# ScalarE in the order of the text during the first block, and the third weight piece transferred ahead of the fourth tile

## The chip, the core and the metric

The kernel runs on one core of a Trainium2 chip, in one launch. The metric is device time in microseconds (us), from start to end of the program. A core has five engines that run side by side, each through a queue of its own: TensorE (PE), VectorE (DVE), ScalarE (ACT), GpSimd (POOL) and SyncE (SP), which here only issues transfers. Engines wait for each other by semaphores; an instruction that waits holds up what is queued behind it on its engine.

## The reference

Three stages, each fed by the one before: an attention with decaying state, a dense MLP, and a mixture of experts.

```python
for t in range(S):                                   # attention: B=4, H=8, S=768, D=48
    cur = np.einsum('bhd,bhe->bhde', u[None] * kt, vt)
    y[:, :, t] = np.einsum('bhd,bhde->bhe', rt, state + cur)
    state = wt[:, :, :, None] * state + np.einsum('bhd,bhe->bhde', kt, vt)
...
h = x @ w_in                                         # MLP: 3072 tokens, 384 -> 2048 -> 384
x = (np.maximum(h, 0.0) + alpha * np.minimum(h, 0.0)) @ w_out
...
expert_idx = np.argmax(x @ w_gate, axis=1)           # 8 experts, 384 -> 1024 -> 384
out[mask] = gate_w[mask, None] * (np.maximum(x[mask] @ w1[e], 0.0) @ w2[e])
```

## The kernel before, in words

**Work.** The 3072 tokens are 24 tiles of 128 (numbered from 0 here, so the fourth tile is tile 3). A block is three tiles, so there are eight blocks. The attention is done tile by tile. A block then goes through the MLP in 16 groups of 128 hidden units: the first product `p1` (L617, into the bank `ph`), ScalarE's `gn` (L620), VectorE's `gt` (L622), then a split of `gt` into a high part `gh` (ScalarE, L628) and a low part `gl` (VectorE, L630), and the second product `p2` (L643, into `py`) two groups later. Each product is made of three TensorE products of high and low parts. There are two `ph` banks, so `p1` of a group waits for `gt` of the group two before.

**Weight pieces.** The MLP's weights come as 16 pieces of 768 KB (numbered from 0, so the third piece is piece 2; even ones are of `w_in`, odd ones of `w_out`). They come packed in pairs of words. SyncE's transfer (L199) brings a piece into `raw` (two buffers; piece 2 goes into a tile of its own, `spare`). ScalarE then rebases it with two instructions (L221, L223); VectorE puts the words together with two (L227, L230, tile `v`); ScalarE casts the high part (L243, `wih` or `woh`); VectorE subtracts it for the low part (L247, `wil` or `wol`). Group f needs pieces 2(f//2) and 2(f//2)+1. In the first block this unpacking runs beside the products, one piece for each group.

**Attention of a tile.** VectorE scans the decays (L297), scans back (L322) and scales `k` (L339); TensorE makes scores (L377) and transposes `k` (L402); ScalarE copies scores out (L385, two copies `at`) and the transposed `k` (L407, `kt`), and makes the state's decays `pm` (L368); GpSimd masks the copies (L389), makes a product `rk` for the *next* tile (L344, L345) and `cv` (L357); VectorE sums `rk` to `c` (L350). TensorE's `kv` (L416, L420) needs `kt`. ScalarE and VectorE split the result into `xth` (L470) and `xtl` (L475).

**What sets the order.** The program is written in slots: `at_slot(s, fn)` hangs a stage onto slot s, and the loop over the groups runs slots 2i and 2i+1 at step i. Slots below zero are the prologue, in which the attention of tiles 0 to 2 and the first pieces are done; `PT0` is its start, `PRO_OPS` and `PRO_MOVED` place attention stages in it, and `PRO_W` places the four stages of a piece (rebase, words, high, low). Engines named in `tc.manual_schedule` keep the order in which the text writes their instructions. On all others the framework's scheduler chooses an order at build time, which is then as fixed as the other. `ORDER0 = None` keeps the text's order on every engine in the prologue, `ORDER1` on TensorE and GpSimd from then on, `ORDER2` on TensorE and VectorE near the expert stage. Nothing is reordered when the program runs.

Of the kernel before, what the change touches and what calls it, by code (L numbers as in the profile page):

```python
# [32 lines left out]
NF1 = DFF // 128  # L33
# [14 lines left out]
LAG = 2  # L48
EPE, EDVE = mybir.EngineType.PE, mybir.EngineType.DVE
EACT, EPOOL = mybir.EngineType.Activation, mybir.EngineType.Pool  # L50


ORDER0 = None
ORDER1 = {EPE, EPOOL}
ORDER2 = {EPE, EDVE}
SWITCH = -6

# [21 lines left out]
PT0 = -100  # L79
# [15 lines left out]

PRO_FILL = 27
GATE_CONST = 34
PRO_W = ((15.75, 17, 20.5, 20.6), (19.64, 19.65, 24.3, 24.4), (24.2, 24.3, 100, 101))
PRO_WARM = ((9.6, 6), (11.5, 3), (14.8, 4), (15.65, 3), (21.55, 4), (22, 5))


def s_tile(i):

    blk, j = divmod(i, NB)
    return 2 * NF1 * blk - 10 - (2 * NF1 * (NB - 1 - j)) // NB
# [3 lines left out]
def attention_mlp_moe(ctx, tc, dmaj, tmaj, ub, alpha, w_in, w_out, w_gate, w_gate_b, wexp, out):  # L109
    nc = tc.nc  # L110
    vec, act, pool, pe, sp = nc.vector, nc.scalar, nc.gpsimd, nc.tensor, nc.sync
    order = ExitStack()
# [20 lines left out]
    def load_tile(i):  # L133
        if i < NB:
            both = wp.tile([128, DMW + TMW], F32, tag="W", name="both")
            dm, tm = both[:PR, :DMW], both[:, DMW:]
            if i == 0:
                sp.dma_start(out=dm[:, 1024:], in_=dmaj[i, :, 1024:])
                sp.dma_start(out=dm[:, :1024], in_=dmaj[i, :, :1024])
            else:  # L140
                sp.dma_start(out=dm, in_=dmaj[i])
        else:
            dm = ap.tile([PR, DMW], F32, tag="dm", name="dm")
            tm = ap.tile([128, TMW], F32, tag="tm", name="tm")
            sp.dma_start(out=dm, in_=dmaj[i])
        sp.dma_start(out=tm, in_=tmaj[i])
        dm_t[i], tm_t[i] = dm, tm
# [45 lines left out]
    def wl_dma(j):  # L193
        g, kind = j // 2, j % 2
        if j == 2:
            raw = spare_t[0][:, 1024:2560].bitcast(U32).rearrange("p (n c) -> p n c", c=2)
        else:
            raw = rp.tile([128, 768, 2], U32, tag="raw", name="raw")
        sp.dma_start(  # L199
            out=raw, in_=(w_in if kind == 0 else w_out)[g].bitcast(U32).rearrange("p (n c) -> p n c", c=2)  # L200
        )
        raw_t[j] = raw
# [422 lines left out]
    def p1_out(blk, f):  # L625
        gt = g_t[(blk, f)]
        gh = mp.tile([128, BN], F32R, tag="gh", name="gh", bufs=3)
        act.copy(gh, gt)  # L628
        gl = mp.tile([128, BN], F32R, tag="gl", name="gl", bufs=3)
        vec.tensor_tensor(out=gl, in0=gt, in1=gh.bitcast(F32), op=ALU.subtract)  # L630
        g_t[(blk, f)] = (gh, gl)
# [19 lines left out]
    def p2_out(blk):  # L651
        x2 = mp.tile([128, NB, DM], F32, tag="x2", name="x2", bufs=1)
        for j in range(NB):
            (vec.tensor_copy if j == 1 else act.copy)(x2[:, j, :], y_t[blk][j])
        sp.dma_start(
            out=x2d[BN * blk : BN * (blk + 1), :].rearrange("(j p) d -> p j d", p=128),
            in_=x2,
        )
        return x2
# [64 lines left out]
    def early_table():  # L724
        ti = counts("e")
        vec.tensor_scalar(ti, ti, UNIT.bit_length() - 1, None, op0=ALU.arith_shift_right)
        tf = scratch([1, E], F32, name="tf_e")
        vec.tensor_copy(tf, ti)
        inc = cumulate("e", tf, E)
        yield from unit_table("e", inc, None, iou[:, :EARLY, :], EARLY, E)  # L730
        mn = scratch([1, 1, E + 1], F32, name="mn")
        vec.tensor_scalar(mn, inc, float(EARLY), None, op0=ALU.min)
        tk = scratch([1, E], F32, name="tk")
        vec.tensor_tensor(out=tk, in0=mn[:, 0, 1:], in1=mn[:, 0, :E], op=ALU.subtract)
        rt["taken"] = tk
# [145 lines left out]
    def b_tr(u, q):  # L881
        d = un[u]
        hs = d.pop(("hs", q))
        pt = ps_a.tile([128, 2, 128], F32, tag="pa", name="pht")
        for m in range(2):
            pe.transpose(pt[:, m, :], hs[:, 128 * m : 128 * m + 128], ident)
        pt = pt.rearrange("p m t -> p (m t)")
        gh = qp.tile([128, 256], F32R, tag="gh2", name="ghb", bufs=4)
        act.copy(gh, pt)
        gl = qp.tile([128, 256], F32R, tag="gl2", name="glb", bufs=4)  # L890
        vec.tensor_tensor(out=gl, in0=pt, in1=gh.bitcast(F32), op=ALU.subtract)
        d["g", q] = (gh, gl)
# [15 lines left out]
    def u_out(u):  # L908
        d = un.pop(u)
        for j in range(d["nt"]):  # L910
            ys = qp.tile([128, DM], F32, tag=f"ys{j}", name=f"ys{j}")
            g = d["meta"][:, j, 1:2].bitcast(F32)
            if j == 0:
                act.activation(ys, d["o"][j], AF.Copy, scale=g)  # L914
            else:
                vec.tensor_scalar(ys, d["o"][j], g, None, op0=ALU.mult)
            pool.indirect_dma_start(  # L917
                out=out,
                out_offset=bass.IndirectOffsetOnAxis(ap=d["meta"][:, j, 0:1], axis=0),
                in_=ys,  # L920
                in_offset=None,
                bounds_check=NT - 1,
                oob_is_err=False,
            )
# [20 lines left out]
    def at_slot(s, fn):  # L945
        todo.setdefault(s, []).append(fn)

    def at_slots(s, stages):

        def stage():  # L950
            for _ in stages:
                at_slots(s + 1, stages)
                return

        at_slot(s, stage)

    def run_slot(s):
        for fn in todo.pop(s, ()):
            fn()
# [17 lines left out]
    for i in range(1, NTILE):  # L977
        at_slot(s_tile(i - 2) + 7 if i > NB + 1 else PT0 + 0.1 * i, lambda i=i: load_tile(i))
        if i == NB - 1:
            at_slot(PT0 + 0.1 * i, lambda: wl_dma(0))  # L980
            at_slot(PT0 + 0.1 * i, lambda: wl_dma(1))
            at_slot(PT0 + 0.1 * i, spare)
            at_slot(PT0 + 0.5, lambda: wl_dma(2))
    for j in range(NWL):
        if j < len(PRO_W):
            s = [PT0 + t for t in PRO_W[j]]
        else:
# [32 lines left out]
    for i in range(len(steps) + LAG):  # L1020
        if i == 0:
            order.close()
            tc.no_sync_barrier()
            order.enter_context(tc.manual_schedule(engines=ORDER1))
        if i == NM + SWITCH:
            order.close()
            ctx.enter_context(tc.manual_schedule(engines=ORDER2))
        if i < len(steps):
            kind, b, f = steps[i]
            {"m": p1, "A": u_p1, "B": b_p1}[kind](b, f)  # L1030
        if 0 < i <= len(steps) and steps[i - 1][0] == "B":
            b_tr(*steps[i - 1][1:])
        run_slot(2 * i)
        if i < NM:
            p1_out(*steps[i][1:])
        if i >= LAG:
            kind, b, f = steps[i - LAG]
            {"m": p2, "A": u_p2, "B": b_p2}[kind](b, f)
            if kind == "m" and f == NF1 - 1:
                x2 = p2_out(b)  # L1040
                end = gate_block(b, x2, 2 * i + 1)
                if b == NBLK - 2:
                    at_slot(end + 1, lambda: list(early_table()))
                elif b == NBLK - 1:
                    at_slots(end + 1, final_table())
            elif kind != "m" and f == ulen[kind] - 1:
                u_out(b)
        run_slot(2 * i + 1)
# [87 lines left out]
```

## Time and profile before

| what | value |
| --- | --- |
| runs before | 851.88, 850.15, 851.5 us; median 851.5 |
| the profiled execution | 853.78 us, its span 852.1 us |
| TensorE busy | 807.1 us (95%), granted clock 0.975 of full |
| VectorE busy | 595.3 us (70%) |
| ScalarE busy | 393.9 us (46%) |
| GpSimd busy | 285.5 us (34%) |

The span runs from the first to the last instruction; the execution's own time has some 1.7 us around it. The prologue lasts to about 39 us, the first block from there to about 132 us, the blocks after it to about 620, the experts to the end. A share of busy time is a mean over these stages; what a stage costs is read from its own windows and waits. The granted clock is 1.00 at 2.4 GHz and 0.50 at 1.2 GHz.

### The profile page before, as it was taken

The numbers are of one execution on the slowest core, as the hardware profiler recorded it, in microseconds if no ns is written. First come the engines' busy times: TensorE is split into PE (matmuls) and PEld (weight loads), VectorE is DVE, ScalarE is ACT, GpSimd is POOL, SyncE is SP. The second block draws the span as 40 slices with busy tenths as digits, with TensorE's granted clock in tenths as the row PEclk, the third lists the DMA queues.
The fourth block names the chain that finished last, engine by engine and source line by source line (L and its number), as shares of the span: only waits on it lengthen the run. The fifth ranks groups of instructions, "written<-read, shape, count | busy, mean of one in ns | idle before, by whom it ended". The sixth has DMA issues, their size and how long they took to land. (4 is left out here: it accounts for less than half of the span.)

```text
span 852.1 us, 15696 instructions
## 1 busy us (share of the span) xinstructions
PE 807.1 (95%) x6032; PEld 757.4 (89%) x6032; DVE 595.3 (70%) x1129; ACT 393.9 (46%) x746; POOL 285.5 (34%) x326
## 2 busy tenths in 40 slices
PE   7878979999999999999999999999899999999994
PEld 4667969999999899999989899989899999999993
DVE  5798876467957967967966953546855676767761
ACT  2476744434334243243244333355445566665641
POOL 7762132443324233434324331130433232222301
PEclk9789989999999999999999999999999999999998
DMA  9835652222123122124123200065267577686830
GB/s 275 262 108 184 216 175 95 63 72 90 46 93 67 63 66 74 58 73 121 35 68 92 71 2 29 1 239 217 98 239 256 186 245 273 227 289 204 293 104 20
DMA packets 30516, 114.80 MB, mean 135 GB/s; under 512 B 8229, under 2 KB 11592, under 8 KB 30440
## 3 DMA queue, kind: packets, MB, share of 16 engines
q1 hardware_dynamic: 26088, 103.53, 37.7%
q0 software_dynamic: 4352, 10.26, 3.2%
q8 instruction: 48, 0.79, 0.4%
q14 instruction: 28, 0.23, 0.1%
HBM read 104.11 MB, written 10.45 MB: 134 GB/s over the span
## 5 line engine op out<-in xcount | busy, mean ns | idle before, releaser
L617 PE MATMUL ph<-xth,wih 128*128 128x384 f32 x384 | 135.7, 353 | 11.5 <-DVE gt L622 10.6
L643 PE MATMUL py<-woh,gh 128*128 128x384 f32 x384 | 135.5, 353 | 1.1 <-ACT gh L628 1.0
L628 ACT CAST gh<-gt 128x384 fp32r<-128x384 f32 x128 | 65.7, 514 | 148.5 <-DVE gt L622 147.8
L643 PE MATMUL py<-woh,gl 128*128 128x384 f32 x384 | 130.1, 339 | 3.6 <-DVE gl L630 3.6
L617 PE MATMUL ph<-xth,wil 128*128 128x384 f32 x384 | 129.7, 338 | 3.0 <-DVE wil L247 3.0
L617 PE MATMUL ph<-xtl,wih 128*128 128x384 f32 x384 | 129.4, 337 | 0.0
L643 PE MATMUL py<-wol,gh 128*128 128x384 f32 x384 | 129.3, 337 | 0.0
L622 DVE SCALAR_TENSOR_TENSOR gt<-gn,oma_s,ph 128x384 f32<-128x384 f32 x128 | 77.8, 608 | 56.8 <-ACT gn L620 56.5
L630 DVE TENSOR_TENSOR gl<-gt,gh 128x384 fp32r<-128x384 f32 x128 | 85.8, 670 | 33.7 <-ACT gh L628 31.4
L620 ACT ACTIVATE gn<-ph 128x384 f32<-128x384 f32 x128 | 62.6, 489 | 81.7 <-PE ph L617 78.6
L848 DVE SCALAR_TENSOR_TENSOR gl<-ph,gh 128x256 fp32r<-128x256 f32 x96 | 40.4, 422 | 73.9 <-ACT gh L846 70.0
L389 POOL TENSOR_SCALAR_AFFINE_SELECT at<-at 128x512 f32<-128x512 f32 x46 | 36.8, 821 | 159.9 <-ACT at L385 159.9
L617 PEld LDWEIGHTS ph<-xth,wih 128*128 128x128 f32 x384 | 72.5, 189 | 19.1 <-DVE gt L622 14.3
L843 PE MATMUL ph<-xh,w1h 128*128 128x256 f32 x288 | 81.5, 283 | 2.3 <-DVE gl L848 2.3
L843 PE MATMUL ph<-xh,w1l 128*128 128x256 f32 x288 | 81.2, 282 | 0.0
L917 POOL DMA_INDIRECT out<-ys,meta x28 | 28.2, 1009 | 157.2 <-ACT ys L914 100.2
L843 PE MATMUL ph<-xl,w1h 128*128 128x256 f32 x288 | 80.6, 280 | 0.0
L643 PEld LDWEIGHTS py<-woh,gh 128*128 128x128 f32 x384 | 72.8, 190 | 7.9 <-issue 3.4
L643 PEld LDWEIGHTS py<-woh,gl 128*128 128x128 f32 x384 | 72.8, 189 | 4.7 <-DVE gl L630 4.5
L617 PEld LDWEIGHTS ph<-xth,wil 128*128 128x128 f32 x384 | 72.7, 189 | 3.3 <-DVE wil L247 3.3
L518 DVE SCALAR_TENSOR_TENSOR sink<-x,wgb 128x384 f32<-128x384 f32 x120 | 75.3, 663 | 0.1
L643 PEld LDWEIGHTS py<-wol,gh 128*128 128x128 f32 x384 | 72.9, 190 | 0.0
(219 smaller groups left out, 1860.9 us busy)
## 6 DMA issues: line engine op xcount, KB each, us to landing
raw<-w SPq DMA_DIRECT2D x64, 768.0 KB
tm<-tmaj SPq DMA_DIRECT2D x21, 704.0 KB
dm<-dmaj SPq DMA_DIRECT2D x21, 674.2 KB
raw<-w_out SPq DMA_DIRECT2D x8, 768.0 KB
raw<-w_in SPq DMA_DIRECT2D x7, 768.0 KB
x2d<-x SPq DMA_DIRECT2D x8, 576.0 KB
both<-tmaj SPq DMA_DIRECT2D x3, 704.0 KB
wgb<-w_gate_b SPq DMA_DIRECT2D x2, 768.0 KB
```

What stands on the lines that cost most here:

```text
L389: pool.affine_select(out=cx[jj], in_=cx[jj], pattern=[[0, NP], [1, 128]], compare_op=ALU.is_gt, fill=0.0, base=0, channel_multiplier=-1,)
L518: vec.scalar_tensor_tensor(out=sink, in0=x2[:, j, :], scalar=1.0, in1=wgb_t[h][:, e, :], op0=ALU.mult, op1=ALU.mult, accum_out=cx["l"][:, ...
L617: pe.matmul(ph, lhsT=w, rhs=x[:, c, :], start=k == 0, stop=k == 3 * KC - 1)
L620: act.activation(gn, ph, AF.Relu, scale=-1.0)
L622: vec.scalar_tensor_tensor(out=gt, in0=gn, scalar=oma_s[:, f : f + 1], in1=ph, op0=ALU.mult, op1=ALU.add)
L628: act.copy(gh, gt)
L630: vec.tensor_tensor(out=gl, in0=gt, in1=gh.bitcast(F32), op=ALU.subtract)
L643: pe.matmul(y_t[blk][j], lhsT=g[:, sl], rhs=w, start=f == 0 and m == 0, stop=f == NF1 - 1 and m == 2,)
L843: pe.matmul(ph, lhsT=w, rhs=x, start=k == 0, stop=k == 3 * KC - 1)
L848: vec.scalar_tensor_tensor(out=gl, in0=ph, scalar=0.0, in1=gh.bitcast(F32), op0=ALU.max, op1=ALU.subtract)
L917: pool.indirect_dma_start(out=out, out_offset=bass.IndirectOffsetOnAxis(ap=d["meta"][:, j, 0:1], axis=0), in_=ys, in_offset=None, bounds_c ...
```

## The change

ScalarE joins the engines that keep the text's order, for the first 18 steps of the loop (groups 0 to 15 of the first block, and two more); from step NF1 + LAG = 18 on a new set without it holds, as before. Piece 2 is transferred in the slot of pieces 0 and 1, ahead of tile 3, and its cast and its low part are placed in the prologue (24.5 and 24.6), where they were placed in slots 0 and 1 of the loop.

```diff
-ORDER1 = {EPE, EPOOL}
+ORDER1 = {EPE, EPOOL, EACT}
+ORDER_LATER = {EPE, EPOOL}
...
-PRO_W = ((15.75, 17, 20.5, 20.6), (19.64, 19.65, 24.3, 24.4), (24.2, 24.3, 100, 101))
+PRO_W = ((15.75, 17, 20.5, 20.6), (19.64, 19.65, 24.3, 24.4), (24.2, 24.3, 24.5, 24.6))
...
-            at_slot(PT0 + 0.5, lambda: wl_dma(2))
+            at_slot(PT0 + 0.1 * i, lambda: wl_dma(2))
...
+        if i == NF1 + LAG:
+            order.close()
+            order.enter_context(tc.manual_schedule(engines=ORDER_LATER))
```

The line numbers of the changed kernel are one higher than those above up to the step loop. TensorE's order is the same in both programs. On ScalarE the order changes from the start of the first block on; there it stood so before, with `v_487` piece 3 and `v_529` piece 4:

```order
L221 ACTIVATE v_487<-raw 128x768
L223 ACTIVATE raw<-raw 128x768
L221 ACTIVATE v_529<-raw 128x768
L223 ACTIVATE raw<-raw 128x768
L620 ACTIVATE gn<-ph 128x384
L368 ACTIVATE pm<-bmask,ex 112x96 x4
L628 CAST gh<-gt 128x384
L385 COPY at_532<-pa_504 128x512
L243 CAST woh_124<-v_487 128x768
L620 ACTIVATE gn<-ph 128x384
L385 COPY at_535<-pa_505 128x512
L407 COPY kt<-pk 128x448
```

and now, at the same place on ScalarE, with `v_488` piece 3:

```order
L621 ACTIVATE gn<-ph 128x384
L222 ACTIVATE v_488<-raw 128x768
L224 ACTIVATE raw<-raw 128x768
L629 CAST gh<-gt 128x384
L621 ACTIVATE gn<-ph 128x384
L244 CAST woh_124<-v_488 128x768
L222 ACTIVATE v_529<-raw 128x768
L224 ACTIVATE raw<-raw 128x768
L386 COPY at_532<-pa_504 128x512
L386 COPY at_535<-pa_505 128x512
L629 CAST gh<-gt 128x384
L408 COPY kt<-pk 128x448
```

The first `gn` stands ahead of the rebases, the rebase of piece 4 behind the cast of piece 3, and both copies of the scores and `kt` behind that rebase.

Further on ScalarE, at group 6 and tile 4, before (`v_779` is piece 9, `v_847` piece 10):

```order
L628 CAST gh<-gt 128x384
L620 ACTIVATE gn<-ph 128x384
L407 COPY kt<-pk 128x448
L221 ACTIVATE v_847<-raw 128x768
L243 CAST woh_741<-v_779 128x768
L223 ACTIVATE raw<-raw 128x768
```

and now, from `gh` of group 6:

```order
L629 CAST gh<-gt 128x384
L386 COPY at_815<-pa_787 128x512
L386 COPY at_818<-pa_788 128x512
L621 ACTIVATE gn<-ph 128x384
L244 CAST woh_741<-v_779 128x768
L222 ACTIVATE v_847<-raw 128x768
L224 ACTIVATE raw<-raw 128x768
L408 COPY kt<-pk 128x448
```

`kt` of tile 4 moved from behind `gn` to behind the cast of piece 9 and the rebase of piece 10, and the copies of its scores, which stood a group earlier, to behind `gh`.

VectorE is left to the scheduler in both, and its order changes with ScalarE's. At groups 6 and 7, before (`v_743` is piece 8):

```order
L622 SCALAR_TENSOR_TENSOR gt<-gn,oma_s,ph 128x384
L350 TENSOR_REDUCE c<-rk 128x8
L247 TENSOR_TENSOR wil_740<-v_743,wih_739 128x3x256
L227 SCALAR_TENSOR_TENSOR v_779<-v_779,raw 128x768
L630 TENSOR_TENSOR gl<-gt,gh 128x384
L230 SCALAR_TENSOR_TENSOR v_779<-raw,v_779 128x768
```

and now, from the same `gt`:

```order
L623 SCALAR_TENSOR_TENSOR gt<-gn,oma_s,ph 128x384
L248 TENSOR_TENSOR wil_740<-v_743,wih_739 128x3x256
L228 SCALAR_TENSOR_TENSOR v_779<-v_779,raw 128x768
L631 TENSOR_TENSOR gl<-gt,gh 128x384
L231 SCALAR_TENSOR_TENSOR v_779<-raw,v_779 128x768
L623 SCALAR_TENSOR_TENSOR gt<-gn,oma_s,ph 128x384
L351 TENSOR_REDUCE c<-rk 128x8
```

The sum `c` of tile 5 moved behind the low part of piece 8, the words of piece 9 and the next `gt`.

## Rows read from the trace of the kernel before

**Rows 1.** Windows: busy us of each engine, granted clock, DMA share and GB/s.

```profile
10.00:30.00 20.00, 13.69 (x113) 9.09 (x113) 16.79 (x19) 10.04 (x22) 17.27 (x15) 0.78 1.03 286
50.00:115.00 65.00, 56.26 (x379) 50.38 (x381) 56.36 (x77) 45.81 (x79) 22.62 (x20) 0.89 0.54 183
83.00:86.00 3.00, 3.00 (x11) 2.33 (x10) 2.62 (x5) 1.85 (x4) 0.00 (x0) 0.50 0.15 43
132.00:620.00 488.00, 480.89 (x3663) 450.66 (x3662) 347.60 (x810) 189.88 (x409) 161.47 (x204) 1.00 0.26 81
```

**Rows 2.** Waits of TensorE, 38 to 150 us: total, times, longest.

```profile
PE ph L617 <- DVE gt L622: 6.0, 1, 6.0
PE py L643 <- DVE gl L630: 3.6, 1, 3.6
PE ph L617 <- DVE wil L247: 3.0, 1, 3.0
```

**Rows 3.** Timeline of TensorE and ScalarE: start us, duration us, engine, line.

```profile
55.90 0.81 PE L416 MATMUL pv<-st,ident 112*112 112x384 f32 x2
...
57.26 0.42 PE L617 MATMUL ph<-xth,wih 128*128 128x384 f32 x1
...
80.93 0.49 ACT L628 CAST gh<-gt 128x384 fp32r<-128x384 f32 x1
...
81.71 0.51 ACT L407 COPY kt<-pk 128x448 f32<-128x448 f32 x1
...
83.82 1.48 PE L416 MATMUL pv<-st,ident 112*112 112x384 f32 x2
...
86.32 0.42 PE L643 MATMUL py<-woh,gh 128*128 128x384 f32 x1
```

**Rows 4.** Waits of VectorE, 49 to 115 us.

```profile
DVE c L350 <- POOL rk L345: 6.0, 3, 2.1
...
DVE wil L247 <- ACT wih L243: 1.0, 1, 1.0
DVE wol L247 <- ACT woh L243: 0.4, 1, 0.4
```

**Rows 5.** Timeline at the prologue's end; brackets: idle before, and its releaser.

```profile
38.52 0.56 DVE L475 TENSOR_TENSOR xtl<-px,xth 128x384 fp32r<-128x384 f32 x1 [2.95 <-ACT xth L470]
...
39.46 0.91 ACT L221 ACTIVATE v<-spare 128x768 f32<-128x768 f32 x1
```

**Rows 6.** Timeline of VectorE at the first `gt`.

```profile
48.04 0.93 DVE L227 SCALAR_TENSOR_TENSOR v<-v,raw 128x768 uint32<-128x768 uint32 x1
48.89 0.89 DVE L339 TENSOR_TENSOR dm<-dm,rec 112x512 f32<-112x512 f32 x1
49.70 0.60 DVE L622 SCALAR_TENSOR_TENSOR gt<-gn,oma_s,ph 128x384 f32<-128x384 f32 x1
```

**Rows 7.** Timeline of ScalarE: a cast and the rebase behind it.

```profile
54.80 0.83 ACT L243 CAST wih<-v 128x768 fp32r<-128x768 f32 x1
...
56.38 0.91 ACT L223 ACTIVATE raw<-raw 128x768 uint32<-128x768 uint8 x1
```

**Rows 8.** Timeline at group 6, and at the low part of piece 14.

```profile
77.38 0.60 DVE L622 SCALAR_TENSOR_TENSOR gt<-gn,oma_s,ph 128x384 f32<-128x384 f32 x1
...
113.46 0.95 DVE L247 TENSOR_TENSOR wil<-v,wih 128x768 fp32r<-128x768 f32 x1
...
117.59 0.34 PE L617 MATMUL ph<-xth,wil 128*128 128x384 f32 x1
```

**Rows 9.** Timeline of GpSimd: masks of tiles 0, 3 and 4, a product.

```profile
10.89 1.23 POOL L389 TENSOR_SCALAR_AFFINE_SELECT at<-at 128x512 f32<-128x512 f32 x2
...
51.40 4.33 POOL L389 TENSOR_SCALAR_AFFINE_SELECT at<-at 128x512 f32<-128x512 f32 x2 [2.18 <-ACT at L385]
...
75.63 2.32 POOL L389 TENSOR_SCALAR_AFFINE_SELECT at<-at 128x512 f32<-128x512 f32 x2 [13.91 <-ACT at L385]
...
77.92 1.00 POOL L344 TENSOR_TENSOR rk<-tm 128x384 f32<-128x384 f32 x1
```

## The prediction

> **What bounds the kernel now.** I read the windows first. From 132 to 620 us TensorE is busy 480.9 of 488 us at full clock, so whatever the first block loses or saves on TensorE arrives at the end. From 50 to 115 us, the stretch that the change reorders, TensorE has 56.3 of 65 us and VectorE 56.4, nearly as much, while TensorE's granted clock falls to 0.89 [rows 1]. Next come TensorE's waits there: three long ones, 6.0 us for `gt`, 3.6 us for `gl` and 3.0 us for a `wil`, all three products of VectorE [rows 2]. Behind the waits the clock is at its lower level: 0.50, 1.2 GHz, from 83 to 86 us, after the 3.0 us wait [rows 1]. The same product `kv` then takes 2.50 us (83.82 to 86.32) instead of 1.36 us (55.90 to 57.26) [rows 3]. Last, VectorE's own waits from 49 to 115: 6.0 us in three waits of the sum `c` for GpSimd, 1.4 in two of L247 for ScalarE's cast [rows 4]. So VectorE, with ScalarE in front of it, sets the pace while weights are unpacked, and TensorE is held or let go by it. The profiled execution took 853.78 us, 2.3 us over the median of the runs; I work in its times and move the result by that.
>
> **The transfer of the third piece** costs and brings nothing. ScalarE reads that piece at 39.46 us and no wait stands before it: it comes behind `pm` in the order of the prologue, in both kernels [rows 5]. Moved ahead, its 768 KB delay tile 3 by at most 2.75 us, at the 286 GB/s of 10 to 30 us [rows 1]. VectorE's scan of tile 3 and all behind it would slide by that, into a hole of 2.95 us before the last `xtl` of the prologue, which waits for ScalarE [rows 5]. If that hole were not there, the first block would start up to 2.75 us later; I take 0.
>
> **The start of the block: 0.9 us gained, then lost.** ScalarE does `gn` of group 0 ahead of the rebases of pieces 3 and 4. But `gt` of group 0 stands on VectorE behind a scan, its reverse and `k` of tile 4 in both orders. Only L227 of piece 3, 0.93 us, moves from before it to after it [rows 6], so `gt` starts at 48.8 instead of 49.7 and the 6.0 us wait shrinks by 0.9. Then ScalarE's new order takes it back: L243 of piece 3, two rebases and two copies of tile 3 now stand before `gh` of group 1 and `kt` of tile 3. Words of piece 3 end at about 51.6 (from 48.8: `gt` 0.6, L227 0.93, `gl` taken as long as `gt`, L230 as L227, less 0.08 of overlap at each [rows 6]). Cast and rebases take 2.49 us from the cast's start to the last rebase's end (54.80 to 57.29) [rows 7], then two copies, `gh` and `kt` at 0.5 each [rows 3]: `kt` ends at about 56.0, and `kv` of tile 3, at 55.90 now [rows 3], stays where it was.
>
> **The loop of a weight piece.** In the order of the text ScalarE rebases piece j+1 only after it cast piece j, and it casts piece j only when VectorE has put its words together; VectorE's next words wait for those rebases. Two kinds of waits follow on VectorE. (a) Where only `gt` stands between L230 and L247, L247 waits for the cast, as it does now in one place for 0.4 us [rows 4]. In the new order so do six pieces up to the low part of piece 14 (3, 5, 7, 8, 11, 13): 2.4 us. (b) Where L227 of the next piece follows L247 at once (after pieces 3, 7, 8, 13), it waits 2.49 less the cast's 0.83 [rows 7] and L247's 0.95 [rows 8]: 0.7 us, four times, 2.8. Elsewhere work of the attention or a `gl` fills the time. Lower bound: 2.6 together, if VectorE's instructions are as stretched by GpSimd as some are now; upper: 5.2 as counted. I take 5.2, since GpSimd works in only 22.6 of these 65 us [rows 1].
>
> **The sums `c`.** The wait of `c` is the length of GpSimd's chain, two masks (2.32 us in one row, 4.33 in another) and two products of 1.0 each [rows 9], counted from the first copy of the scores, less what VectorE does meanwhile. For tile 4: copies from 54.1, first ready at 54.7, masks to 57.0, products to 59.1; VectorE, with L227, L230 and `gl` from 54.1, reaches `c` at 56.4. It waits 2.7, where it now waits 2.0; I take +0.7 for each of three, 2.1 (bounds: 0, and 2.0 more for a pair of masks that lasts 4.33).
>
> The Trainium skill's page "SBUF — State Buffer" (Who interferes with whom) says that a VectorE instruction with two SBUF inputs contends with a GpSimd instruction that reads SBUF, and one with a single such input does not. The rows are in line with it: a pair of masks took 1.23 us at 10.9, before any piece is unpacked, and 4.33 at 51.4, amid the unpacking [rows 9]. By that rule masks beside a waiting VectorE would go at 1.23; I leave them at 2.32, since words and `gl` stand beside them in the new order.
>
> **Summed at two places.** At `gt` of group 6: -0.9, three waits (a) 1.2, two (b) 1.4, one `c` 0.7: +2.4, from 77.38 to 79.8 [rows 8]. Words of piece 8 end there, cast and rebases of ScalarE come next (2.49), so `gh` of group 6 starts at 82.3 instead of 80.93. Behind it `kt` of tile 4 will stand after the cast of piece 9 and both rebases: 0.5 for `gh`, 0.6 for `gl`, 0.9 for L230, then 2.49 and `kt`'s own 0.51, so it ends at 87.3. Before the change it runs at 81.71, two rows behind `gh` [rows 3]. `kv` of tile 4 starts at 87.35 instead of 83.82, 3.5 us later; at full clock it gives 1.1 of that back (1.36 for 2.50), so TensorE is 2.4 us late at 86.32. At L247 of piece 14: -0.9, -0.6 (`gt` of group 13 comes behind it now), +5.2, +2.1, and -1.4 since L247's present waits are in (a): +4.4, so 117.9 and its end 118.8. TensorE needs it at 117.59 now [rows 8]: 1.3 us late there by VectorE alone, and 2.4 by its own delay if it has caught up nothing. Behind that no wait of the block is in sight, and between the two places I see none that TensorE loses. I take 2.4: 856.2 in the profile's time, **853.9 us** on the scale of the runs.
>
> **Rivals.** (1) Masks go alone: three pairs at 1.23 instead of 2.32 take 3.3 off VectorE, and 2.4 becomes -0.9: 850.6 us. For it: GpSimd's row at 10.9 us; against: what stands beside the masks in the new order. This is what the Trainium skill's rule on the two SBUF inputs would make of it if VectorE stood still there. (2) Faster: where TensorE waits 3.0 us for `wil` and 3.6 us for `gl` [rows 2], VectorE has just been held by `c`. The new order puts L247 of piece 8 ahead of `c` of tile 5, and `gl` of group 11 ahead of `c` of tile 6. Both waits go, and with the first the 1.1 us of `kv` at half clock: 7.7 us. Against that stand the 5.2 us of the loop, if all of them reach TensorE: -2.5, 849.0 us. It decides if VectorE's waits in the loop, `kt` of tile 4 among what is queued behind them, hold TensorE for less than 7.7 in all. Against it: `kt` by itself holds it for 3.5. (3) Slower by more: two of the three pairs of masks at 4.33: 4.0 more on VectorE, 6.4 in all, 857.9. For it: the row of tile 3's masks; against: two pairs in three do not show it. (4) Nothing changes: ScalarE has 19 us idle in these 65 [rows 1], and its order costs nothing unless VectorE waits for it; 851.5.
>
> **Chances and range.** My forecast 0.46, (1) 0.10, (2) 0.25, (3) 0.12, (4) 0.07. A measurement of this kernel tells 0.2%, 1.7 us, from no change; of my forecast's cases (+1.3, where VectorE alone counts, to +4.4, where all of its delay does) about one in six ends within it. So faster 0.25 ((2)), same 0.25 ((1), (4) and 0.08 of the forecast), slower 0.50. The range goes from 847.5, past (2), to 858.5, past (3); the forecast's own is 852.8 to 855.9.
>
> **What would show it.** Right: a wait of TensorE of 3 us or more for `kt` of tile 4 before its `kv`; waits of L227 and L247 on VectorE that sum to 4 us or more, where now 1.4 stand; ScalarE waiting for L230 before most casts; the first long wait of TensorE at 5 us; nothing moved before 38 us. Wrong: TensorE reaching the low part of piece 14 before VectorE does; `c` waits under 1.5 us; a clock that stays at its upper level all through 80 to 118 us, which alone would give up to 4 us.

## The result, and the profile after

| | before | after |
|---|---|---|
| median of 19 runs each, us | 851.36 | 854.74 |
| after / before (95% interval) | | 1.0054 (1.0033 to 1.0076) |
| profiled execution: time, span, granted clock | 853.78, 852.1, 0.975 | 854.29, 852.6, 0.975 |

The changed kernel is slower by 0.54%, 4.6 us, with an interval from 2.8 to 6.5 us. One run of before took 2704.33 us; the ratio goes by the fast runs, without it, and the two medians by themselves differ by 3.4 us. The two profiled executions differ by 0.5 us only, because that of before lies 2.4 us above its median and that of after 0.45 below. Up to the end of the first block the two traces differ by what the runs say: the last product of its MLP ends at 132.42 us before and at 136.09 after (135.76 and 0.33, below), 3.7 us later. By the last product of the whole MLP (583.4 and 586.1 us) the difference is 2.6 us, and behind that the profile of before takes 2.1 us more than that of after, in code that the change does not touch. So I read the first block.

The windows of the changed kernel, in the columns of [rows 1]:

```profile
10.00:30.00 20.00, 14.61 (x120) 10.13 (x117) 16.72 (x19) 10.94 (x23) 16.71 (x15) 0.88 1.02 328
50.00:115.00 65.00, 58.35 (x383) 51.83 (x385) 55.23 (x73) 43.89 (x77) 17.50 (x17) 0.87 0.54 178
132.00:620.00 488.00, 481.83 (x3666) 452.48 (x3663) 346.55 (x810) 192.25 (x416) 159.29 (x203) 1.00 0.26 80
```

What follows the first block can absorb little of its loss: TensorE has 481.8 of 488 us at full clock (480.9 in [rows 1]), and 1.0 us of the 3.7 comes back there. From 50 to 115 us VectorE and ScalarE do less in the same time (55.2 for 56.4 and 43.9 for 45.8).

Waits of the changed kernel (total us, times, longest): TensorE from 38 to 150 us, then VectorE and ScalarE from 49 to 115.

```profile
PE ph L618 <- DVE gt L623: 5.2, 1, 5.2
PE ph L618 <- DVE wil L248: 3.9, 2, 2.6
PE pv L421 <- ACT kt L408: 3.8, 1, 3.8
PE py L644 <- DVE gl L631: 1.0, 2, 0.6
...
DVE c L351 <- POOL rk L346: 4.1, 2, 2.1
DVE v L228 <- ACT raw L224: 2.8, 5, 0.7
DVE wol L248 <- ACT woh L244: 1.5, 4, 0.4
DVE wil L248 <- ACT wih L244: 0.4, 1, 0.4
...
ACT woh L244 <- DVE v L231: 8.9, 5, 2.4
ACT wih L244 <- DVE v L231: 7.7, 5, 2.0
```

Beside [rows 2] the wait for `kt` is new, 3.8 us; the wait of 3.6 for `gl` is gone, and the one for a low part has moved to another piece. On VectorE L228 waits for the rebase, which it did not do in [rows 4], and L228 and L248 together lose 4.7 us where 1.4 stood. The waits of `c` are three as before; the third, at 116.74, is outside this list's window. ScalarE stands 16.6 us at ten casts for the words: cast, rebase and words go round in turn.

Places on the timeline, engines mixed (start, duration, in brackets idle time and what ended it):

```profile
49.21 0.60 DVE L623 SCALAR_TENSOR_TENSOR gt<-gn,oma_s,ph 128x384 f32<-128x384 f32 x1
...
55.79 0.95 PE L417 MATMUL pv<-st,ident 112*112 112x384 f32 x2
...
59.71 0.55 DVE L351 TENSOR_REDUCE c<-rk 128x8 f32<-128x384 f32 x1 [2.01 <-POOL rk L346]
...
84.03 0.90 PE L417 MATMUL pv<-st,ident 112*112 112x384 f32 x2
...
88.20 0.52 ACT L408 COPY kt<-pk 128x448 f32<-128x448 f32 x1
...
88.77 1.81 PE L421 MATMUL pv<-tm,kt 128*112 128x96 f32 x8 [3.83 <-ACT kt L408]
90.28 0.67 PE L644 MATMUL py<-woh,gh 128*128 128x384 f32 x1
...
116.66 1.18 POOL L313 TENSOR_TENSOR dm<-dm,ex 112x512 f32<-112x512 f32 x1
117.80 1.69 POOL L358 TENSOR_TENSOR cv<-tm,c 128x256 f32<-128x256 f32 x2
...
116.74 0.55 DVE L351 TENSOR_REDUCE c<-rk 128x8 f32<-128x384 f32 x1 [2.08 <-POOL rk L346]
117.21 2.02 DVE L248 TENSOR_TENSOR wil<-v,wih 128x768 fp32r<-128x768 f32 x1
...
119.28 0.44 PE L618 MATMUL ph<-xth,wil 128*128 128x384 f32 x1 [2.63 <-DVE wil L248]
...
135.76 0.33 PE L644 MATMUL py<-woh,gl 128*128 128x384 f32 x1
```

Against [rows 3, 6, 8]: `gt` of group 0 is 0.5 us earlier, `kv` of tile 3 where it was (55.79 for 55.90), the product behind `kv` of tile 4 4.0 us later (90.28 for 86.32), TensorE's read of the low part of piece 14 1.7 later (119.28 for 117.59), the end of the block 3.7 later. TensorE reaches that read at 116.65 (119.28 less its wait), 0.9 ahead of before: all that the wait for `kt` cost has come back by then. The 3.6 us for `gl` are gone, and so is before's stretch at the lower clock about them (0.50 from 110.0 to 116.8). Then 2.63 us of it are lost again, to VectorE: there `c` waits for GpSimd right ahead of the low part, and the low part itself takes 2.02 us.

The clock explains the last step. From 120.90 to 124.30, right behind the 2.63 us wait, it is at its lower level (0.50, 1.2 GHz) with TensorE busy all the time; before it was at 1.00 in this window. The lines show this stretch and the one about the wait for `kt` in the changed kernel, and last the one about the wait for `gl` in the kernel before:

```profile
86.80:93.60 6.80, 4.83 (x19) 4.74 (x20) 5.13 (x8) 5.11 (x11) 2.67 (x3) 0.50 0.41 129
120.90:124.30 3.40, 3.40 (x24) 3.02 (x17) 3.03 (x5) 1.63 (x3) 0.41 (x4) 0.50 0.43 119
...
110.00:116.80 6.80, 5.13 (x38) 4.31 (x42) 6.80 (x11) 3.38 (x5) 1.80 (x1) 0.50 0.33 116
```

From 120.90 on that is 1.7 us of full-clock work in 3.4: with the 1.7 at the read it makes 3.4 of the 3.7.

### The profile page after: what moved, and what is told of

It reads as the page before. It is cut to its first block, busy times and chain, and to the rows that moved or that the text cites. A ratio compares the mean times of both kernels' runs of the same rounds, so it can differ in the third digit from the quotient of the medians.

```text
span 852.6 us, 15703 instructions
## 1 busy us (share of the span) xinstructions
PE 811.1 (95%) x6032; PEld 761.0 (89%) x6032; DVE 598.0 (70%) x1129; ACT 393.0 (46%) x746; POOL 280.6 (33%) x326
## 5 line engine op out<-in xcount | busy, mean ns | idle before, releaser
L631 DVE TENSOR_TENSOR gl<-gt,gh 128x384 fp32r<-128x384 f32 x128 | 87.3, 682 | 31.2 <-ACT gh L629 23.9
L849 DVE SCALAR_TENSOR_TENSOR gl<-ph,gh 128x256 fp32r<-128x256 f32 x96 | 40.4, 421 | 72.4 <-ACT gh L847 70.5
L918 POOL DMA_INDIRECT out<-ys,meta x28 | 30.3, 1083 | 159.8 <-ACT ys L915 98.7
```

Of the source, the lines that this page charges most:

```text
L849: vec.scalar_tensor_tensor(out=gl, in0=ph, scalar=0.0, in1=gh.bitcast(F32), op0=ALU.max, op1=ALU.subtract)
L918: pool.indirect_dma_start(out=out, out_offset=bass.IndirectOffsetOnAxis(ap=d["meta"][:, j, 0:1], axis=0), in_=ys, in_offset=None, bounds_c ...
```

## The experiments

Each kernel from e1 on was timed in five rounds (6 to 12 runs) beside the kernel before, on the same chip; e1 to e4, e5 to e8 and e9 to e12 ran on three different chips, and the row "after" is the comparison above. The table gives the ratio to before, and three lengths of the one profiled execution in us. "Group 2" is the start of the MLP's first product of group 2, the one behind TensorE's first long wait; "to the end" goes from there to the end of the block's last product; "weight loop" goes from the start of L228 of piece 3 to the end of L248 of piece 14. A profile's start is its own: "group 2" differs by up to 2.6 us between kernels with the same order on VectorE there (after and e3), so the two lengths are what I compare. In before, e2, e4, e6 and e12 the loop starts 2.3 to 4.9 us ahead of group 2, in the others within about 1 us of it.

| kernel | ratio (95% interval) | group 2 | to the end | weight loop |
|---|---|---|---|---|
| before | 1 | 50.4 | 82.1 | 66.4 |
| after | 1.0054 (1.0033 to 1.0076) | 49.9 | 86.2 | 69.5 |
| e1 order alone | 1.0042 (1.0028 to 1.0056) | 49.4 | 87.2 | 70.5 |
| e2 piece alone | 1.0023 (1.0006 to 1.0040) | 51.6 | 81.8 | 67.8 |
| e3 `kt` early | 1.0055 (1.0034 to 1.0076) | 47.3 | 85.8 | 69.8 |
| e4 rebase early | 1.0091 (1.0067 to 1.0115) | 50.1 | 88.3 | 75.7 |
| e5 order in three steps | 0.9991 (0.9971 to 1.0011) | 47.6 | 81.7 | 66.8 |
| e6 order behind them | 1.0043 (1.0025 to 1.0062) | 49.4 | 84.0 | 70.5 |
| e7 cast behind rebase | 1.0027 (1.0012 to 1.0041) | 48.4 | 83.4 | 67.7 |
| e8 cast on GpSimd | 1.0059 (1.0039 to 1.0079) | 47.7 | 86.6 | 67.3 |
| e9 `rk` early | 1.0080 (1.0058 to 1.0103) | 54.0 | 88.8 | 69.0 |
| e10 e5 without the piece | 0.9993 (0.9970 to 1.0016) | 46.8 | 80.4 | 64.2 |
| e11 e5 with `rk` early | 1.0007 (0.9986 to 1.0027) | 53.1 | 79.4 | 64.5 |
| e12 before, `rk` early | 0.9996 (0.9978 to 1.0014) | 53.9 | 78.2 | 64.5 |

My theory: the text's order on ScalarE puts casts and rebases in step with VectorE's words, and `kt` behind them. Rivals: the moved transfer is the loss (R-B), or TensorE's stretches at the lower clock alone (R-A).

**e1 and e2: the two halves of the change.** e1 is the changed kernel without the move of the piece:

```diff
-PRO_W = (..., (24.2, 24.3, 24.5, 24.6))
+PRO_W = (..., (24.2, 24.3, 100, 101))
...
-            at_slot(PT0 + 0.1 * i, lambda: wl_dma(2))
+            at_slot(PT0 + 0.5, lambda: wl_dma(2))
```

> ScalarE keeps the order of the text in the first block, as in the changed kernel, but the third weight piece (piece 2) is transferred behind the fourth tile and cast where the kernel before has it. Theory (the order is the loss: casts, rebases and kt stand behind other work of ScalarE and hold VectorE's words and TensorE's kv): slower than before by 3 to 6 us, like the changed kernel; VectorE's waits for the rebase (L228) and the cast (L248) between 49 and 115 us sum to 4 us or more (1.4 before), and TensorE waits 3 to 4 us for kt of tile 4 near 88 us. Rival R-B (the moved transfer is the loss): within 0.2% of before. Rival R-A (only TensorE's stretches at the lower clock differ): the same two waits as before, and a first block that ends earlier or later by the difference of its stretches at the lower clock alone.

e2 is the changed kernel with the order of before:

```diff
-ORDER1 = {EPE, EPOOL, EACT}
+ORDER1 = {EPE, EPOOL}
```

> The other half of the change alone: piece 2 is transferred ahead of the fourth tile and cast in the prologue, and ScalarE is ordered by the scheduler as before. Theory (the transfer costs and brings nothing): 0 within 0.3% of before; the first block ends within 1 us of 132.4; waits for L228 and L248 between 49 and 115 us below 2 us in sum. Rival R-B (the transfer is the loss): +3 to +6 us, with the first chunks of tile 3 or the first product of the MLP (39.2 us before) later by as much.

The order alone costs 0.42%, with the waits of the changed kernel; TensorE's and VectorE's in e1:

```profile
PE pv L421 <- ACT kt L408: 4.3, 2, 3.8
...
DVE v L228 <- ACT raw L224: 2.8, 5, 0.7
DVE wol L248 <- ACT woh L244: 1.5, 4, 0.4
DVE wil L248 <- ACT wih L244: 0.4, 1, 0.4
```

The piece alone leaves the stretch to the end as it was (81.8), though VectorE's L228 and L248 wait 4.0 us there, twice what I expected as the most. It is 0.23% slower, and the interval, 0.06 to 0.40%, leaves out zero only just. In its one profile TensorE waits more at the start, for an `xtl` and the first `gt`, where starts differ from profile to profile:

```profile
PE ph L618 <- DVE gt L623: 5.7, 3, 3.9
...
PE ph L618 <- DVE xtl L476: 4.1, 1, 4.1
```

R-B falls for the loss in the loop. That the piece costs 1 to 2 us under the scheduler's order at the start is not excluded; with the text's order there (e5 against e10) it cost nothing that can be measured.

**e5 and e6: where the order costs.** e5 ends the text's order on ScalarE behind the third step of the loop; e6 begins it there.

```diff
-        if i == NF1 + LAG:
+        if i == 3:
             order.close()
             order.enter_context(tc.manual_schedule(engines=ORDER_LATER))
```

```diff
-            order.enter_context(tc.manual_schedule(engines=ORDER1))
+            order.enter_context(tc.manual_schedule(engines=ORDER_LATER))
+        if i == 3:
+            order.close()
+            order.enter_context(tc.manual_schedule(engines=ORDER1))
         if i == NF1 + LAG:
```

> The changed kernel with ScalarE in the order of the text for the first three MLP steps alone (up to the copies of kt of tile 3); from the fourth step on the scheduler orders ScalarE, as in the kernel before. Theory (the loss is made in the loop of the weight pieces, from 50 us on): from the first product of group 2 to the end of the block 82 us as before and in the run with the piece alone (81.8 to 82.1), not 85.8 to 88.3; the time within 0.3% of before. Rival (the loss is made in the first steps, by kt of tile 3 and the placing of piece 2): 85 us or more, and +0.4% or more.

> The other part alone: ScalarE is ordered by the scheduler in the first three MLP steps and keeps the order of the text from the fourth step to the end of the first block. Theory: 85.5 to 87 us from the first product of group 2 to the end of the block, waits of VectorE for L228 and L248 of 4 us or more in sum, the time +0.3 to +0.6% over before. Rival (the first steps): 82 us and the time of before.

The loss lies behind the third step: e5 has none, e6 0.43%, close to e1's. VectorE's waits in e5, from 49 to 115 us, are 2.3 us for rebase and cast:

```profile
DVE c L351 <- POOL rk L346: 2.8, 2, 2.0
DVE v L228 <- ACT raw L224: 1.4, 3, 0.7
DVE wol L248 <- ACT woh L244: 0.6, 2, 0.4
...
DVE wil L248 <- ACT wih L244: 0.3, 1, 0.3
```

e6 has 3.4 (I had expected 4 or more) and 84.0 us to the end (85.5 expected). Its weight loop is 70.5, as long as e1's, but 3.2 us of that lie ahead of group 2; from group 2 to the end of the low part of piece 14 it has 67.3 us, the changed kernel 69.4, e5 66.7 and before 64.1.

**e3: the visible wait taken away.** The copy of `kt` is written one slot (half a step) earlier:

```diff
-                at_slot(s0 + OPS[n], fn)
+                at_slot(s0 + OPS[n] - (n == "ko" and i < 6), fn)
```

> The changed kernel with the step that holds kt moved one slot earlier for tiles 0 to 5, so that kt of tile 4 stands right behind the score copies on ScalarE, ahead of gn of group 7, of the cast and of the rebases. Theory: the 3.8 us wait of TensorE at kv of tile 4 goes (below 0.5), p2 of group 6 starts at 87 to 88 instead of 90.28; but the words loop of VectorE keeps its 4.7 us of waits for L228 and L248, so that the wait for the low part of piece 14 (2.63) grows by what was gained, and the block ends 0 to 2 us earlier than the changed kernel's 136.1. Rival (kt is the whole loss): the block ends at 132.5, and the time is that of before. Rival R-A (the clock): the time follows the stretches at the lower clock, not the wait.

`kv` of tile 4 now starts without a wait, as the timeline of TensorE shows, but the time is that of the changed kernel, and so is the weight loop:

```profile
80.99 0.90 PE L417 MATMUL pv<-st,ident 112*112 112x384 f32 x2
81.90 1.03 PE L421 MATMUL pv<-tm,kt 128*112 128x96 f32 x8
```

Its waits on TensorE from 38 to 150 us are now for the unpacked weights, the high part too:

```profile
PE ph L618 <- DVE wil L248: 4.3, 3, 2.6
...
PE py L644 <- DVE gl L631: 3.0, 4, 1.4
...
PE ph L618 <- ACT wih L244: 2.1, 3, 1.6
```

So the largest new wait on TensorE was not what set the end. R-A falls too: this profile has only 6.8 us at the lower clock between 40 and 150 us, against 20.4 in the changed kernel's, with 0.5 us less from group 2 to the end: TensorE is busy for 2.1 us less of that stretch (74.8 for 76.9), and waits for 1.7 more.

**e4 and e7: rebase ahead of cast.** e4 writes each rebase from piece 3 on one slot (half a step of the loop) earlier; e7 only swaps a cast and the rebase of the next piece, which stand side by side.

```diff
             s = [2 * j - WL_OFF + n for n in range(4)]
+            s[0] -= 1
```

```diff
         for n, fn in enumerate(wl_stages(j)):
-            at_slot(s[n], fn)
+            if n == 0 and held:
+                at_slot(s[0], fn)
+                at_slot(*held.pop())
+            elif n == 2 and 2 < j < NWL - 1:
+                held.append((s[n], fn))
+            else:
+                at_slot(s[n], fn)
```

> The changed kernel with the rebases of pieces 3 to 15 written one slot earlier, so that on ScalarE a piece's rebase stands ahead of the cast of the piece before it. Theory (lockstep of cast, rebase and words): VectorE's waits for the rebase and the cast between 49 and 115 us fall from 4.7 to below 2.5 us, the low part of piece 14 is done 2 us earlier, TensorE's 2.63 us wait for it falls below 1, and the block ends 1.5 to 3 us ahead of the changed kernel's 136.1; the 3.8 us wait for kt of tile 4 stays. Rival (the words loop isn't the bound): the waits fall and the end doesn't move. Rival (ScalarE then stands at the transfers): ScalarE waits for the raw weights' transfer 3 us or more, and the time is that of the changed kernel or more.

> The changed kernel with one swap: on ScalarE the cast of a piece (from piece 3 on) stands directly behind the rebase of the next piece instead of directly ahead of it; gn, gh and kt keep their places. Theory (cast ahead of rebase makes the lockstep): the waits for the rebase (L228) fall from 2.8 us to below 1.5, those for the cast (L248) rise from 1.9 us by up to 0.8 per piece, the stretch from group 2 to the end of the block is 83 to 85 us instead of 86.2, and the time lies 1 to 3 us below the changed kernel's. Rival (it is not their order but that both stand behind gn and gh in a fixed round): 86 us or more, as the changed kernel; ScalarE waits for raw's transfer 2 us or more in sum.

e4 came out as its last rival had it, and worse: ScalarE stands 9.1 us at the transfers of the raw weights and 14.7 at `gh` for `gt`, and VectorE waits 7.2 us for rebases, not less than 2.8. VectorE and ScalarE in e4:

```profile
DVE v L228 <- ACT raw L224: 7.2, 6, 2.1
...
ACT gh L629 <- DVE gt L623: 14.7, 9, 5.3
ACT v L222 <- DMA raw<-w_out: 6.8, 2, 5.5
ACT v L222 <- DMA raw<-w_in: 2.3, 2, 1.3
```

e7 gives back half: 0.27% instead of 0.54%, 83.4 us to the end instead of 86.2, a loop of 67.7 instead of 69.5. How it does so was not what I expected: the wait for rebases stayed (2.7), that for casts, which I had put higher, went, and ScalarE now stands 9.8 us at transfers. VectorE and ScalarE in e7:

```profile
DVE v L228 <- ACT raw L224: 2.7, 2, 1.3
...
ACT v L222 <- DMA raw<-w_out: 6.3, 3, 2.4
ACT v L222 <- DMA raw<-w_in: 3.5, 2, 2.3
```

The intervals of e7 and the changed kernel overlap, so the time alone does not tell how much the pair's order is worth; the loop points the same way.

**e8: the cast off ScalarE.** From piece 3 on the cast goes to GpSimd.

```diff
-            act.copy(hi, v)
+            (pool.tensor_copy(out=hi, in_=v) if j > 2 else act.copy(hi, v))
```

> The changed kernel with the casts of pieces 3 to 15 on GpSimd instead of ScalarE, so that ScalarE no longer waits for the words at a cast and goes on to the next rebase. GpSimd takes 1.0 to 1.1 us for a 128x384 multiply, so a cast of 128x768 is estimated at 1.1 to 2.2 us against 0.83 on ScalarE. Theory (ScalarE standing at the casts, 16.6 us in sum, holds rebases and kt): the waits of VectorE for the rebase fall below 1 us, those for the cast are 0.3 to 1.4 us a piece; the 3.8 us wait for kt of tile 4 falls below 2.5; the stretch from group 2 to the end of the block 82 to 86 us. Rival (VectorE's own work fills the loop): the waits move to the cast and the stretch stays at 86 us or more.

The rebases come in time (L228 waits 1.3) and the loop is shorter, 67.3. But the stretch to the end is 86.6 us, as the rival had it: the casts now queue behind GpSimd's other work, as at piece 14, and the time is no better:

```profile
106.66 4.44 POOL L358 TENSOR_TENSOR cv<-tm,c 128x256 f32<-128x256 f32 x2
111.06 1.22 POOL L390 TENSOR_SCALAR_AFFINE_SELECT at<-at 128x512 f32<-128x512 f32 x2
112.23 0.82 POOL L244 CAST wih<-v 128x768 fp32r<-128x768 f32 x1
...
113.09 1.75 DVE L248 TENSOR_TENSOR wil<-v,wih 128x768 fp32r<-128x768 f32 x1 [2.24 <-POOL wih L244]
```

What it gained up to piece 14 it lost behind it; one cause seen there is a wait of TensorE of 2.6 us for an `xtl`.

**e9, e11, e12: the sums `c`.** In the three kernels (after, e5, before) `rk` of tiles 4 to 7 is written ahead of the masks of the tile before, into time in which GpSimd was idle.

```diff
-                at_slot(s0 + OPS[n], fn)
+                at_slot(s_tile(i - 1) if n == "rk" and NB < i < 8 else s0 + OPS[n], fn)
```

> The changed kernel with the two multiplications that make rk for tiles 4 to 7 written ahead of the masks of the tile before on GpSimd (which stood idle there, waiting for the score copies), so that VectorE's sum c finds rk ready. Theory (a wait of c for rk, 2.1 us, stands directly ahead of the low part of piece 14 and is the last part of the loss): the waits of c between 49 and 115 us fall from 4.1 us to below 0.5, the low part of piece 14 is done 2 to 3 us earlier from the start of group 2, TensorE's 2.63 us wait for it falls below 1, and the stretch from group 2 to the end of the block is 83 to 85 us instead of 86.2; the time 1 to 3 us below the changed kernel's. Rival (the weight loop takes up what c gives back): the waits of c go and the stretch stays at 86. Rival (masks behind rk hold kv): TensorE waits for the masks 1 us or more at kv of tiles 3 and 4.

> The whole change with the text order cut to the first three MLP steps, and rk ahead of the masks for tiles 4 to 7: a candidate against both kernels. Theory: the waits of c for rk go (2.8 us in the run without the rk edit), the stretch from group 2 to the end of the block falls below 81.5 us, and the time lies 1 to 3 us below before (0.9965 to 0.999). Rival (the stretch is bound by TensorE and by the casts, not by c): 81.5 to 82.5 us and within 0.2% of before.

> The kernel before with rk ahead of the masks for tiles 4 to 7 and nothing else: the cover of VectorE's waits for rk in the kernel before, tested by itself. In its profile two waits of TensorE behind them (3.0 for the cast of wih and 3.6 for gl) are the ones that the rival of 849.0 us lets go. Theory: they shrink by 1 to 3 us in sum, the block ends 1 to 2.5 us earlier, the time is 0.997 to 0.999 of before. Rival (c was covered there): 82 us from group 2 to the end of the block, and no change.

In none of the three did the time fall. VectorE is ordered by the scheduler in all of them, and it answered the earlier `rk` by moving `c` of tile 4 ahead of `gt` of group 0, where it waits for that very `rk`. VectorE in e12:

```profile
49.92 0.55 DVE L350 TENSOR_REDUCE c<-rk 128x8 f32<-128x384 f32 x1 [2.82 <-POOL rk L345]
...
53.25 0.61 DVE L622 SCALAR_TENSOR_TENSOR gt<-gn,oma_s,ph 128x384 f32<-128x384 f32 x1
```

TensorE's first wait grows from 6.0 [rows 2] to 9.1 us, and group 2 starts 3.6 later than before. In the loop behind it e11 and e12 have no other wait of `c`; e12's loop is 1.9 us shorter than before's, e11's 2.3 shorter than e5's. But e10 has as short a loop (64.2) with 4.3 us of such waits, so what they are worth stays open. In sum nothing is won. e9 starts late too, in its profile also by a wait of 5.0 us for an `xtl` in group 0. Its two waits of `c` in the loop are 0 and 1.4 us for the changed kernel's 2.06 and 2.08, and the loop is 69.0 for 69.5: where ScalarE keeps the text's order, the weights take up nearly all that `c` gives back, as the first rival had it. Why its stretch to the end is still 2.6 us longer (88.8) was not followed; a wait of 2.9 for an `xtl` behind piece 14 is part of it. The edit for tiles 5 to 7 alone, without tile 4, was not tried.

**e10: the start without the piece.** e5 with the two edits of e1.

> The text order on ScalarE for the first three MLP steps alone, without the moved transfer and placing of piece 2. With the piece it was 0.9991 of before (0.9971 to 1.0011). Theory (the piece brings nothing, the order of the first steps brings about 0.5 to 1 us at the first gt, the loop is left as it was): 0.9975 to 1.001, and 81.5 to 82.5 us from group 2 to the end of the block. Rival (the moved piece is worth its part at the start only together with the order): 1.001 to 1.004, with the first wait of TensorE for gt of group 0 at 6 us as before.

0.9993, with 80.4 us to the end: as e5 within their intervals, with or without the moved piece. Neither is shown to beat the kernel before. Its waits for L228 and L248 are 3.1 us, nearly e6's 3.4, without e6's loss: the sum of these waits alone does not tell what a kernel loses.

## Why the prediction was right, and where it was not

The time came out 0.8 us above the forecast, slower than before by an amount that the measurement tells from nothing. Step by step:

- **The transfer of the third piece, 0.** Right beside the text's order at the start (e5 against e10). Alone, under the scheduler's order, it measured +0.23%, an amount that I had not priced.
- **The start, 0.9 gained and lost again.** The mechanism was right: the first wait went from 6.0 to 5.2 us (5.1 forecast), `gt` from 49.70 to 49.21 (48.8 forecast; the block's first product starts 0.4 later in this profile, 39.58 for 39.20), and `kv` of tile 3 stayed at its place. With the loop left to the scheduler (e5, e10) the kernel is at 0.9991 and 0.9993: what the start brings does not show in the time.
- **The loop, (a) and (b), 5.2.** L228 waits 2.8 us in five places (2.8 in four forecast), L248 1.9 in five (2.4 in six). The rise over before, 1.4, is 3.3. The result goes with this part: all runs with the text's order in the loop and the cast in its place have loops of 69.0 us or more, those with the scheduler's 67.8 or less (67.3 or more against 66.7 or less, counted from group 2). That the two waits are how the loop gets longer is argued and not shown: e2 and e10 wait 4.0 and 3.1 us there and lose nothing behind group 2, e6 waits 3.4 and loses 0.43%.
- **The sums `c`, +2.1.** This step failed. The waits did not grow: 2.01, 2.06 and 2.08 us, 6.1 in all for the 6.0 of [rows 4]. For tile 4 GpSimd's products were done at 59.7 (59.1 forecast), but VectorE reached `c` only at 57.7 (56.4 forecast), and so found as short a wait as before.
- **`kt` of tile 4 and the 1.1 us given back by the clock.** The wait was forecast and came, `kv` starting at 88.77 after 3.83 us of it (88.20 for `kt`, 86.8 forecast for its start, 87.3 less 0.51). But the product behind it was 4.0 us late and not 2.4, for the most part because `kt` was done 1.4 us later than forecast (88.72 for 87.3; `gh` of group 6, ahead of it on ScalarE, started 0.7 later, 82.99 for 82.3). The 1.1 did not come as reckoned either: I had let all of `kv` wait for `kt`, 1.36 us at full clock, while its first part (L417) ran ahead of the wait, and the second part alone (L421) took 1.5 from 88.77 at the lower clock (0.50 from 86.8 to 93.6).
- **What the end hangs on.** I took TensorE's delay at tile 4, 2.4, as the one that lasts, and saw no wait behind it that it loses. That step failed twice over: e3 takes the delay away without changing the time, and in the changed kernel TensorE has made up all of it at 116.65. The wait of 3.6 us for `gl` between the two places, which my own rival (2) lets go, did go. TensorE reaches the low part of piece 14 before VectorE does, which the prediction had named as a sign against it. What lasts is VectorE's lateness there: the end of that low part was forecast 4.4 later (118.8) and is 4.8 later (119.23, from 114.41). That the two are so near is in part chance: the 2.1 of the sums did not come, and the low part took 2.02 us for 0.95, 1.1 that I had not counted. That makes TensorE 1.7 late, where I had given 1.3 by VectorE alone, and the wait is followed by 3.4 us at the lower clock, which I had not counted: 1.7 more. These two terms, and not the 2.4, are 3.4 of the 3.7 at the end of the block.

The forecast's +2.4 is half of the measured 4.6 and below its interval (2.8 to 6.5), and that the time still came within 0.8 us is partly luck: the step that was meant to carry it does not, and the one that does was counted but put aside. That rebases behind casts make about half of the loss rests on e7 alone, whose interval overlaps the changed kernel's, and is not shown. That the rest is casts and rebases in a fixed place among `gn` and `gh` fits e5 and e6, and was not separated further.

## What to carry to other kernels

An order written out for one engine should be tried on a stretch at a time: here three steps of it cost nothing and the steps behind them all that was lost. Where two engines hand a buffer back and forth, ask which work stands ahead of the hand-over in each queue, and measure the loop by its own first and last instruction; the largest new wait on the bottleneck engine (3.8 us) can be one whose removal changes nothing, because a second queue is late too. And an edit that makes an input ready earlier can move its consumer ahead in a scheduled queue, where it waits again.

## What the runs showed that I had not expected

- VectorE's subtraction of two 128x768 operands took 2.02 us at 117.21, 0.95 at [rows 8], with GpSimd at its multiplications from 116.66 to 119.49 in the first case and idle in the second. The sum `c`, with one input, ran beside the same multiplications at 116.74 and took 0.55, as in the kernel before at 44.02, where GpSimd stood idle. This is the rule of the Trainium skill, "SBUF — State Buffer" (Who interferes with whom), that a VectorE instruction with two SBUF inputs contends with a GpSimd instruction that reads SBUF, and one with at most one such input, outside VectorE's 2-port modes, does not. The trace agrees, and here the contention stood on the instruction that TensorE was waiting for.
- A cast of 128x768 took GpSimd 0.82 us in e8, as long as ScalarE (0.83 at [rows 7]); I had estimated 1.1 to 2.2 from its 128x384 products. At piece 14 it was the queue ahead of the cast, and not its speed, that held VectorE.
